# Summing second products over pairs of units, another decoding table, and waits by tile, in a fused attention and two-mixture kernel

## The chip, the cores and the metric

The kernel runs on one core of one Trainium2 chip. The core has five engines with a program of their own each: TensorE (PE in the profile; its weight loads are PEld), VectorE (DVE), ScalarE (ACT), GpSimd (POOL) and SyncE (SP), which issues transfers. What counts is the device time of one execution in microseconds (us), the median over several runs.

## What is computed

An attention over clustered heads gives x (1536 tokens by 512). Two mixtures follow, and the change is in the first:

```python
def _moe_ref(x, w_in, w_out, a, b):      # x 1536 x 512, w_in 512 x 2048, w_out 2048 x 512, weights float64
    h = x @ w_in
    h2 = h * h
    h3 = h2 * h
    P = a[0] + a[1] * h + a[2] * h2 + a[3] * h3
    Q = 1.0 + np.abs(b[0]) * np.abs(h) + np.abs(b[1]) * h2
    g = P / (Q + 1e-06)
    return (g @ w_out).astype(np.float32)
```

The second mixture (`_moe2_ref`) takes that result: a gate over 8 experts, normalised in 8 rounds, then for each expert `relu(x @ w1) @ w2`, weighted by the gate and summed. Every product is made as three matmuls of high and low parts (`mm3`, lines 778 to 781), so that about float32 precision is reached.

## The kernel before, in words

**Stages.** The attention fills the first 287 us of the profiled execution, the first mixture 287 to 581 us, the second mixture the rest. The order of the instructions on each engine is the order in which the Python code issues them; nothing reorders them.

**Units, chunks, ticks.** The 2048 hidden columns of the first mixture are cut into 8 units of 256 (`NU1`). The 1536 tokens are cut into 3 chunks of 512, and a unit's columns into 2 blocks of 128 (`FT`), so each unit has 6 (`PER`) blocks h of 128 x 512, and the mixture 48 (`N1`). The loop over t (lines 1199 to 1239) makes one tick for each: TensorE makes the block h of number n = t (`stage1`, 12 matmuls of 512 columns into a PSUM bank; there are three such banks, pool `ps_1`) and, four ticks behind (`LAG1`), two blocks y of a second product (`stage2`, 6 matmuls each). A tick is thus 24 matmuls. What is issued in which tick stands in the table `plan`, which lines 1157 to 1196 fill.

**The activation.** A block h is read by four ScalarE operations one tick later (`act_b`, lines 820 to 823: h2, q, uu, ww), by two of GpSimd (lines 824 and 825, the polynomial into uu), one of VectorE (`act_q`, L829) and by ScalarE's logarithm and exponentials (`act_r`, lines 833 to 837), which put 1/Q into h's own bank. Another tick later VectorE runs `act_steps`: L843 makes the high part of g (hh), L844 and L847 the residue res, L850 the low part hl. L850 is the last reader of h's bank. For every third n above 3, GpSimd does that last step instead (L848), on a copy rr of the reciprocal.

**The sums.** For each y block of a unit VectorE adds the bank to the accumulator in SBUF (`out1`, L882), two such adds a tick; for unit 0 ScalarE copies (L880). When the last unit has been added, ScalarE and GpSimd split the sum into the high and low parts XH and XL, the second mixture's input.

**Decoding.** The weights come as float64, loaded as pairs of 32-bit words (`load_w`, line 606; one staging buffer for w_in and one for w_out) and decoded into high and low float32 parts by `split_w`. A unit has two weight tiles, (unit, 0) of w_in and (unit, 1) of w_out, each 128 x 1024. Six steps, one per tick, make one tile: a on ScalarE (L649), b on VectorE (L652), c on VectorE (L655), d a copy on ScalarE (L660) and two VectorE operations (L661, L662), e and f on GpSimd (L665, L668). A tile is begun every three ticks, so steps a to c of one tile fall between d to f of the one before.

**The order within a tick** on VectorE is this line, where `outs` are the adds, a, b, c, d the four steps of `act_steps`, and w the decoding step:

```python
            steps = outs[:1] + [a] + firsts + [b] + outs[1:] + [c] + p.get("w", []) + [d]
```

**Pools.** Buffers come from pools that lie on a stack, and a new pool may lie where a closed one lay. The pools of the first mixture (`tp`, `accp`, `hb`, `ps_1`, `ps_2`, `ps_q` and others) are opened after those of the attention are closed.

Of the kernel before, what the change touches and what calls it, by code (L numbers as in the profile page):

```python
# [9 lines left out]
F32 = mybir.dt.float32  # L10
# [23 lines left out]
def kernel(  # L34
# [15 lines left out]
    nc = tc.nc  # L50
# [43 lines left out]
    def left(name, bufs):  # L94
        return ctx.enter_context(tc.tile_pool(name=name, bufs=bufs))
# [577 lines left out]
    LASTK = 2 * NT * (NPR - 1)  # L673
    early = {0: [lambda: (load_w(0, 0), load_w(0, 1))]}
# [28 lines left out]
    tp = mctx.enter_context(tc.tile_pool(name="tp", bufs=2))  # L703
# [4 lines left out]
    sg2 = right(ctx, "sg2", 1)  # L708
    ps_1 = psum(ctx, "ps_1", 3)
# [79 lines left out]
    def stage1(n, ui, c, f):  # L789
        m = units[ui][0]  # L790
        if f == 0:
            hid[ui, c] = (
                hb.tile([P, FT, 512], F32R, tag="hh", name=f"hh_{ui}_{c}"),
                hb.tile([P, FT, 512], F32R, tag="hl", name=f"hl_{ui}_{c}"),
            )
# [43 lines left out]
    def act_steps(n):  # L839
        ps, q0, _, uu, _, gh, gl, *rr = act.pop(n)  # L840
        res = tt("res", n, 2)
# [13 lines left out]

    def stage2(ui, c, i):
        m, e, u = units[ui]
# [3 lines left out]
        if m == 0:  # L861
            first, last = u == 0, u == NU1 - 1
            ps = ps_2.tile([P, 512], F32, tag="2", name=f"y_{ui}_{c}_{i}")
            for f in range(FT):
                mm3(
                    ps, wh[:, f, sl], wl[:, f, sl], gh[:, f], gl[:, f],
                    f == 0, f == FT - 1,
                )
            late.append(lambda: out1(ps, c, i, first, last))
            return  # L870
# [289 lines left out]
    for ui in range(NO):  # L1160
        m = units[ui][0]
        for c in range(NCH):
            for f in range(FT):
                n = ui * PER + c * FT + f
                t = n + m * SHIFT
# [111 lines left out]
```

## Time and profile before

| | |
|---|---|
| median of 3 runs | 1602.87 us (1601.77 to 1603.26) |
| the profiled execution | 1603.93 us |
| its span in the profile | 1602.2 us |
| TensorE busy | 1543.4 us, 96% |
| VectorE busy | 1208.8 us, 75% |
| GpSimd busy | 814.9 us, 51% |
| ScalarE busy | 682.3 us, 43% |

The span is the time from the first to the last recorded instruction; the time of the execution has 1.7 us more around it. In the trace, a group of rows names the line of the code, the engine, and the tiles written and read; a bracket behind an instruction tells how long its engine sat idle before it and which instruction ended that. Matmuls overlap: one of 512 columns is shown with 0.39 us, and the next begins 0.22 to 0.23 us after it.

### The profile page before, as it was taken

The numbers are of one execution on the slowest core, as the hardware profiler recorded it, in microseconds if no ns is written. First come the engines' busy times: TensorE is split into PE (matmuls) and PEld (weight loads), VectorE is DVE, ScalarE is ACT, GpSimd is POOL, SyncE is SP. The second block draws the span as 40 slices with busy tenths as digits, with TensorE's granted clock in tenths as the row PEclk, the third lists the DMA queues.
The fourth block names the chain that finished last, engine by engine and source line by source line (L and its number), as shares of the span: only waits on it lengthen the run. The fifth ranks groups of instructions, "written<-read, shape, count | busy, mean of one in ns | idle before, by whom it ended". The sixth has DMA issues, their size and how long they took to land.

```text
span 1602.2 us, 21123 instructions
## 1 busy us (share of the span) xinstructions
PE 1543.4 (96%) x7780; PEld 1354.3 (85%) x7780; DVE 1208.8 (75%) x1963; ACT 682.3 (43%) x1292; POOL 814.9 (51%) x725
## 2 busy tenths in 40 slices
PE   5999999799999999999999999999999999999999
PEld 4888887577777788889899999989999998999997
DVE  5888888899999966978666766676676666667666
ACT  4999888797777751222221212222121222212121
POOL 5577674698777885243533443353344335334420
PEclk8999999899999999999999999999999999999999
DMA  8555542212112000010110110011011001101102
GB/s 183 135 115 134 132 111 83 74 54 79 53 53 79 14 27 27 27 41 27 40 40 27 40 40 27 27 40 40 27 41 40 27 27 40 40 27 40 40 1 79
DMA packets 70951, 87.96 MB, mean 55 GB/s; under 512 B 29793, under 2 KB 48321, under 8 KB 70849
## 3 DMA queue, kind: packets, MB, share of 16 engines
q1 hardware_dynamic: 70848, 86.63, 19.2%
q8 instruction: 61, 1.00, 0.3%
q14 instruction: 42, 0.34, 0.1%
HBM read 62.97 MB, written 3.19 MB: 41 GB/s over the span
## 4 chain that ended last, share of the span: by engine, by line
PE 77%; DVE 14%; issue 4%; ACT 3%; POOL 2%; DMA 0%; SPq 0%; ACTq 0%; POOLq 0%
PE y L780 12%; PE y L781 12%; PE y L779 12%; PE m L781 9%; PE m L779 9%; PE m L780 9%; PE pt L440 2%; DVE acc L882 2%; PE v L462 2%; PE h L779 1%; PE v L463 1%; PE h L781 1%; PE h L780 1%; DVE ptl L450 1%; PE s L415 1%
## 5 line engine op out<-in xcount | busy, mean ns | idle before, releaser
L896 DVE SCALAR_TENSOR_TENSOR acc<-y,gate,acc 128x512 f32<-128x512 f32 x348 | 260.7, 750 | 189.2 <-PE y L781 188.1
L1013 POOL TENSOR_TENSOR rl<-sg,rh 128x512 fp32r<-128x512 f32 x29 | 45.9, 1584 | 535.4 <-ACT rh L1005 535.4
L781 PE MATMUL y<-wh,gl 128*128 128x512 f32 x696 | 273.1, 392 | 0.0
L780 PE MATMUL y<-wl,gh 128*128 128x512 f32 x696 | 272.8, 392 | 0.0
L779 PE MATMUL y<-wh,gh 128*128 128x512 f32 x696 | 270.6, 389 | 0.0
L1074 ACT ACTIVATE gh<-u 128x384 fp32r<-128x384 f32 x58 | 30.5, 527 | 425.8 <-DVE u L1099 425.8
L781 PEld LDWEIGHTS y<-wh,gl 128*128 128x128 f32 x696 | 130.4, 187 | 27.4
L780 PEld LDWEIGHTS y<-wl,gh 128*128 128x128 f32 x696 | 130.6, 188 | 25.1
L779 PEld LDWEIGHTS y<-wh,gh 128*128 128x128 f32 x696 | 130.7, 188 | 24.7
L779 PE MATMUL h<-XH,wh 128*128 128x512 f32 x264 | 107.0, 405 | 24.3 <-DVE hl L850 24.3
L1090 ACT COPY c<-m 128x384 f32<-128x384 f32 x58 | 27.9, 481 | 220.7 <-PE m L781 220.7
L450 DVE TENSOR_TENSOR ptl<-pt,pth 128x384 fp32r<-128x384 f32 x192 | 97.4, 548 | 29.3 <-ACT pth L449 29.1
L1075 DVE SCALAR_TENSOR_TENSOR gl<-v,gh 128x384 fp32r<-128x384 f32 x174 | 117.1, 673 | 0.0
L1074 ACT ACTIVATE gh<-v 128x384 fp32r<-128x384 f32 x174 | 91.2, 524 | 60.6 <-DVE v L1113 27.5
L781 PE MATMUL h<-XH,wl 128*128 128x512 f32 x264 | 104.4, 395 | 1.1 <-POOL wl L668 1.1
L780 PE MATMUL h<-XL,wh 128*128 128x512 f32 x264 | 104.4, 395 | 0.0
L637 POOL TENSOR_TENSOR wl<-sg,wh 128x512 fp32r<-128x512 f32 x70 | 98.7, 1411 | 5.8
L421 DVE TENSOR_REDUCE nm<-s 128x1 f32<-128x768 f32 x96 | 91.1, 949 | 6.7 <-PE s L416 5.9
L440 PE MATMUL pt<-ident,pr 128*128 128x128 f32 x576 | 85.2, 280 | 8.5 <-DVE ptl L450 8.1
L449 ACT CAST pth<-pt 128x384 fp32r<-128x384 f32 x192 | 82.7, 482 | 23.8 <-PE pt L440 22.7
L429 ACT ACTIVATE pr<-s,nm 128x768 f32<-128x768 f32 x96 | 87.7, 914 | 1.6 <-DVE nm L421 1.1
L824 POOL TENSOR_TENSOR uu<-uu,h 128x512 f32<-128x512 f32 x48 | 67.6, 1409 | 38.5 <-ACT uu L822 38.5
(226 smaller groups left out, 4271.4 us busy)
## 6 DMA issues: line engine op xcount, KB each, us to landing
sg<-in_moe_w_dram SPq DMA_DIRECT2D x64, 512.0 KB, 3.6
stg<-in_moe_w_in_dram SPq DMA_DIRECT2D x8, 1024.0 KB, 5.3
stg<-in_moe_w_out_dram SPq DMA_DIRECT2D x8, 1024.0 KB, 4.8
st<-HQK SPq DMA_DIRECT2D x16, 384.0 KB, 3.9
st<-LQK SPq DMA_DIRECT2D x32, 192.0 KB, 4.3
st<-HQK SPq DMA_DIRECT2D x32, 192.0 KB, 4.5
qk<-in_q_dram SPq DMA_DIRECT2D x16, 192.0 KB, 3.0
qk<-in_k_dram SPq DMA_DIRECT2D x16, 192.0 KB, 3.9
```

The lines of the kernel that those rows point to most:

```text
L421: nc.vector.tensor_reduce(nm, ps[:, :, :HS], axis=AX.XY, op=ALU.max, negate=True)
L429: nc.scalar.activation(pr, ps[:, :, :HS], AF.Exp, bias=nm, accum_out=rss[n][:, x : x + 1])
L440: nc.tensor.transpose(ps[:, i * P : (i + 1) * P], pv_[:, j * P : (j + 1) * P], ident)
L449: nc.scalar.copy(th[:, jj, :], ps[:, :HS])
L450: nc.vector.tensor_tensor(tl[:, jj, :], ps[:, :HS], th[:, jj, :].bitcast(F32), op=ALU.subtract)
L637: gt(wl[:, c], raw[:, c], wh[:, c].bitcast(F32), op=ALU.subtract)
L779: nc.tensor.matmul(ps, ah, bh, start=first, stop=False)
L780: nc.tensor.matmul(ps, ah, bl, start=False, stop=False)
L781: nc.tensor.matmul(ps, al, bh, start=False, stop=last)
L896: nc.vector.scalar_tensor_tensor(a, ps, p, a, op0=ALU.mult, op1=ALU.add)
L1074: nc.scalar.activation(gh[:, f], c, AF.Relu)
L1075: soon.append(lambda: nc.vector.scalar_tensor_tensor(gl[:, f], c, 0.0, gh[:, f].bitcast(F32), op0=ALU.max, op1=ALU.subtract))
```

## The change

1. Every pool that is opened by `left`, `right` and `psum`, and those of the mixture opened directly, get `reuse_waits="tile"`: the first user of a buffer in a new pool then waits for the users of the tiles that lay there, not for those of the whole pool.
2. Units 2 to 7 are taken in pairs, in groups of 12 ticks (`GP`): for each chunk the four h blocks of both units, then the next chunk's. A y block is summed in PSUM over both units, 12 matmuls (`units_sum`), so that there is one y block and one add per tick. Units 0 and 1 stay as they were. A pair's y stand 6 ticks or more behind its h, the last ones in ticks 50 to 53. In tick 54 the second products and the gate's step come before the block h.
3. The table `DECODE` gives for each weight tile the ticks of its six steps, counted from the group's first tick: b and c in one tick, d in the next. The first row is for the first group, the second for the others. From tick 12 on the decoding step comes behind step d of the activation. Decoding ends in tick 37 in place of 41.
4. Buffers: weights have a second pool `wx` for some tiles, the hidden blocks a fourth buffer `hx`, `res` has one buffer in place of two, and the scratch for transfers 1024 in place of 8192 bytes.
5. In the second mixture the gate's factors (`factors`) stand two ticks later, one piece of `pieces_s` one tick later, and the pools `wq` and `cp` are opened at tick 55 instead of 50. The first two weight tiles of the second mixture are split at ticks 46 and 48.

The core of the diff:

```diff
-        return ctx.enter_context(tc.tile_pool(name=name, bufs=bufs))
+        return ctx.enter_context(tc.tile_pool(name=name, bufs=bufs, reuse_waits="tile"))
...
+        pool, bufs = (wx, 1 + i) if ui < NU1 and (ui % 4 > 1 if i else ui % 3 == 2) else (wp, 2)
...
+            pool = hx if m == 0 and len(hid) % 4 == 3 else hb
...
-        res = tt("res", n, 2)
+        res = tt("res", n, 1)
...
+    def units_sum(us, c, i):
+
+        sl = slice(i * P, (i + 1) * P)
+        ps = ps_2.tile([P, 512], F32, tag="2", name=f"y_{us[0]}_{c}_{i}")
+        ks = [(ui, f) for ui in us for f in range(FT)]
+        for ui, f in ks:
+            gh, gl = hid[ui, c]
+            wh, wl = weights[ui, 1]
+            mm3(
+                ps, wh[:, f, sl], wl[:, f, sl], gh[:, f], gl[:, f],
+                (ui, f) == ks[0], (ui, f) == ks[-1],
+            )
+        late.append(lambda: out1(ps, c, i, us[0] == 0, us[-1] == NU1 - 1))
...
+    GP = 2 * PER
+    DECODE = (
+        ((5, 6, 6, 7, 8, 9), (9, 10, 10, 11, 12, 13), (7, 8, 8, 9, 10, 11), (12, 13, 13, 14, 15, 16)),
+        ((3, 4, 4, 5, 6, 7), (8, 9, 9, 10, 11, 12), (6, 7, 7, 8, 9, 10), (11, 12, 12, 13, 14, 15)),
+    )
+    for g in range(NU1 // 2):
+        for x in range(GP):
+            n = t = g * GP + x
+            if g:
+                c, f = divmod(x, 2 * FT)
+                at(t, "s1", (n, 2 * g + f // FT, c, f % FT))
+                at(t - f + 2 * FT + 2 + f, "y", ((2 * g, 2 * g + 1), c, f))
+            else:
+                c, f = divmod(x % PER, FT)
+                at(t, "s1", (n, x // PER, c, f))
+                for i in range(KC * f // FT, KC * (f + 1) // FT):
+                    at(t + LAG1, "y", ((x // PER,), c, i))
+            at(t + 1, "b", n)
+            at(t + 2, "d", n)
+        t = g * GP
+        if g + 1 < NU1 // 2:
+            for when, (ui, i) in zip(DECODE[g > 0], ((2, 0), (3, 0), (2, 1), (3, 1))):
+                at(t + when[0], "P", (2 * g + ui, i, [t + x for x in when]))
...
-            steps = outs[:1] + [a] + firsts + [b] + outs[1:] + [c] + p.get("w", []) + [d]
+            w = p.get("w", [])
+            steps = outs[:1] + [a] + firsts + [b] + outs[1:]
+            steps += [c] + w + [d] if t < GP else [c, d] + w
...
-        for a in p.get("s1", ()):
-            stage1(*a)
+        if t != N1 + 6:
+            firsts_()
         for fn in p.get("g", ()):
             fn()
...
+        seconds()
+        if t == N1 + 6:
+            firsts_()
...
-    for x, fn in zip((3, 3, 4, 4, 5, 6, 7, 8, 8, 9, 10, 11, 12, 13, 14, 15), factors()):
+    for x, fn in zip((5, 5, 6, 6, 7, 8, 9, 10, 10, 11, 11, 12, 13, 14, 15, 16), factors()):
```

How this moves instructions at two places. A row names the line, the operation, the tile written and the tiles read with their numbers, and what the instruction waits for; `DMAHW..` are transfers, the other names engines. First ScalarE at the start of the first mixture, where it goes from the attention's last copy to the first block h; before:

```order
L500 COPY x1f_7_3805<-v_31_3987 64x384
L649 ACTIVATE mag_1_0_4020<-stg_1_0_3902 128x1024 [waits DMAHW3_49]
L820 ACTIVATE h2_0_4076<-h_0_0_0_4063 128x512 [waits DMAHW2_49,DMAHW4_49,DMAHW1_49,DMAHW5_49,DVE_49,DMAHW6_49,PE_49,Pool_49]
L821 ACTIVATE q_0_4079<-h_0_0_0_4063,cf_158 128x512
L822 ACTIVATE uu_0_4077<-h_0_0_0_4063,cf_158 128x512
L823 ACTIVATE ww_0_4078<-h_0_0_0_4063,cf_158 128x512
L833 ACTIVATE h_0_0_0_4063<-q_0_4079,lnb_163 128x512 [waits DVE_49,Activation_49]
```

With the change (line 826 is what line 820 was, and so on):

```order
L500 COPY x1f_7_3805<-v_31_3987 64x384
L650 ACTIVATE mag_1_0_4020<-stg_1_0_3902 128x1024 [waits DMAHW3_49]
L826 ACTIVATE h2_0_4082<-h_0_0_0_4069 128x512 [waits PE_49]
L827 ACTIVATE q_0_4085<-h_0_0_0_4069,cf_158 128x512 [waits Activation_49]
L828 ACTIVATE uu_0_4083<-h_0_0_0_4069,cf_158 128x512
L829 ACTIVATE ww_0_4084<-h_0_0_0_4069,cf_158 128x512
L839 ACTIVATE h_0_0_0_4069<-q_0_4085,lnb_163 128x512 [waits DVE_49,Activation_49]
```

The first activation of block 0 waits for the matmuls alone, where it waited for six transfers, VectorE, GpSimd and TensorE.

Then VectorE in the middle of the mixture, in tick 20 and the start of tick 21 before (q_20 and res_18, res_19 tell the block; y_2_1 and y_2_2 are blocks of unit 2):

```order
L847 TENSOR_TENSOR res_18_5032<-uu_18_4964,q_18_4966 128x512 [waits DVE_49]
L661 TENSOR_SCALAR mag_4_0_4925<-top_4_0_4926 128x1024
L662 SCALAR_TENSOR_TENSOR mag_4_0_4925<-stg_4_0_4769,mag_4_0_4925 128x1024 [waits DVE_49]
L882 TENSOR_TENSOR acc_4059<-y_2_2_0_5070,acc_4059 128x512 [waits PE_49]
L843 TENSOR_TENSOR hh_3_0_4948<-uu_19_5015,h_3_0_1_5001 128x512 [waits Activation_49,Pool_49]
L829 SCALAR_TENSOR_TENSOR q_20_5069<-h2_20_5066,cf_158,q_20_5069 128x512 [waits Activation_49]
L844 SCALAR_TENSOR_TENSOR q_19_5017<-q_19_5017,hh_3_0_4948 128x512 [waits DVE_49]
L882 TENSOR_TENSOR acc_4059<-y_2_2_1_5077,acc_4059 128x512 [waits PE_49]
L847 TENSOR_TENSOR res_19_5091<-uu_19_5015,q_19_5017 128x512 [waits DVE_49]
L652 TENSOR_SCALAR mag_4_1_5086<-mag_4_1_5086 128x1024
L850 TENSOR_TENSOR hl_3_0_4949<-res_19_5091,h_3_0_1_5001 128x512 [waits DVE_49]
L882 TENSOR_TENSOR acc_4059<-y_2_2_2_5126,acc_4059 128x512 [waits PE_49]
```

With the change, two ticks of the same kind of stretch (blocks 26 to 28; lines 653 and 656 are b and c, 662 and 663 are d, 892 the add, 853 res, 856 hl):

```order
L853 TENSOR_TENSOR res_26_5429<-uu_26_5362,q_26_5364 128x512 [waits DVE_49]
L856 TENSOR_TENSOR hl_5_0_5347<-res_26_5429,h_5_0_0_5348 128x512 [waits DVE_49]
L653 TENSOR_SCALAR mag_6_0_5426<-mag_6_0_5426 128x1024
L656 SCALAR_TENSOR_TENSOR top_6_0_5427<-stg_6_0_5175,mag_6_0_5426 128x1024 [waits DMAHW0_49,DVE_49]
L892 TENSOR_TENSOR acc_4065<-y_2_2_2_5467,acc_4065 128x512 [waits PE_49]
L849 TENSOR_TENSOR hh_5_0_5346<-uu_27_5408,h_5_0_1_5394 128x512 [waits Activation_49,Pool_49]
L835 SCALAR_TENSOR_TENSOR q_28_5466<-h2_28_5463,cf_158,q_28_5466 128x512 [waits Activation_49]
L850 SCALAR_TENSOR_TENSOR q_27_5410<-q_27_5410,hh_5_0_5346 128x512 [waits DVE_49]
L853 TENSOR_TENSOR res_27_5480<-uu_27_5408,q_27_5410 128x512 [waits DVE_49]
L662 TENSOR_SCALAR mag_6_0_5426<-top_6_0_5427 128x1024
L663 SCALAR_TENSOR_TENSOR mag_6_0_5426<-stg_6_0_5175,mag_6_0_5426 128x1024 [waits DVE_49]
L892 TENSOR_TENSOR acc_4065<-y_2_2_3_5515,acc_4065 128x512 [waits PE_49]
```

The decoding step has moved behind hl, b and c stand together, and one add stands in a tick instead of two.

## Rows read from the trace of the kernel before

**Rows 1.** The page, part 1: busy time, share of the span, instructions.

```profile
PE 1543.4 (96%) x7780; PEld 1354.3 (85%) x7780; DVE 1208.8 (75%) x1963; ACT 682.3 (43%) x1292; POOL 814.9 (51%) x725
```

**Rows 2.** Busy time by stretch; columns: PE, PEld, DVE, ACT, POOL, clock, DMA share, GB/s.

```profile
336.77:358.53 21.76, 21.76 (x98) 18.02 (x96) 21.00 (x26) 21.57 (x35) 21.45 (x13) 1.00 0.16 49
358.53:542.96 184.43, 170.72 (x722) 134.84 (x721) 183.89 (x241) 138.60 (x212) 147.72 (x92) 0.99 0.17 58
542.96:581.10 38.14, 38.14 (x170) 31.49 (x169) 32.40 (x52) 27.92 (x46) 33.95 (x26) 1.00 0.04 15
690.07:1600.00 909.93, 908.42 (x4543) 820.35 (x4542) 616.39 (x1003) 193.21 (x373) 340.57 (x304) 1.00 0.11 35
```

**Rows 3.** Waits in 287.28 to 581.1: us in total, times, longest.

```profile
PE h L779 <- DVE hl L850: 24.3, 21, 9.5
```

**Rows 4.** TensorE in time: start, duration, operation [idle before <- releaser].

```profile
307.85 0.79 PE L779 MATMUL h<-XH,wh 128*128 128x512 f32 x1 [9.51 <-DVE hl L850]
...
457.49 0.50 PE L779 MATMUL h<-XH,wh 128*128 128x512 f32 x1 [1.34 <-DVE hl L850]
...
463.45 0.50 PE L779 MATMUL h<-XH,wh 128*128 128x512 f32 x1 [0.21 <-DVE hl L850]
...
469.03 0.39 PE L779 MATMUL h<-XH,wh 128*128 128x512 f32 x1
```

**Rows 5.** VectorE in time, ticks of the steady part.

```profile
454.98 1.86 DVE L652 TENSOR_SCALAR mag<-mag 128x1024 uint32<-128x1024 uint32 x1
456.76 0.67 DVE L850 TENSOR_TENSOR hl<-res,h 128x512 fp32r<-128x512 f32 x1
...
459.82 0.67 DVE L882 TENSOR_TENSOR acc<-y,acc 128x512 f32<-128x512 f32 x1
460.42 0.67 DVE L847 TENSOR_TENSOR res<-uu,q 128x512 f32<-128x512 f32 x1
461.01 1.79 DVE L655 SCALAR_TENSOR_TENSOR top<-stg,mag 128x1024 uint32<-128x1024 uint32 x1
462.73 0.67 DVE L850 TENSOR_TENSOR hl<-res,h 128x512 fp32r<-128x512 f32 x1
...
466.97 0.68 DVE L661 TENSOR_SCALAR mag<-top 128x1024 uint32<-128x1024 uint32 x1
467.68 2.20 DVE L662 SCALAR_TENSOR_TENSOR mag<-stg,mag 128x1024 f32<-128x1024 uint32 x1
469.81 0.68 DVE L882 TENSOR_TENSOR acc<-y,acc 128x512 f32<-128x512 f32 x1
```

**Rows 6.** One line's instructions: shortest/median/longest ns, first and last start.

```profile
L655 DVE SCALAR_TENSOR_TENSOR top<-stg,mag x16: 1214/1786/2866, 271.9 to 534.9; 128x1024 uint32<-128x1024 uint32 x16
...
L662 DVE SCALAR_TENSOR_TENSOR mag<-stg,mag x16: 1226/2198/2202, 275.6 to 541.6; 128x1024 f32<-128x1024 uint32 x16
...
L824 POOL TENSOR_TENSOR uu<-uu,h x48: 1270/1308/2271, 299.7 to 576.7; 128x512 f32<-128x512 f32 x48
...
L665 POOL TENSOR_TENSOR top<-top,wh x16: 2358/2402/2859, 278.1 to 546.3; 128x1024 f32<-128x1024 f32 x16
```

**Rows 7.** GpSimd in time, the same part.

```profile
453.89 2.40 POOL L665 TENSOR_TENSOR top<-top,wh 128x1024 f32<-128x1024 f32 x1
```

**Rows 8.** ScalarE, VectorE and GpSimd in time at the mixture's start.

```profile
297.76 0.60 ACT L820 ACTIVATE h<-h 128x512 f32<-128x512 f32 x1 [6.79 <-issue]
...
297.04 0.56 DVE L511 TENSOR_TENSOR XL<-x1f,XH 128x384 fp32r<-128x384 f32 x1
298.94 0.76 DVE L829 SCALAR_TENSOR_TENSOR q<-h,cf,q 128x512 f32<-128x512 f32 x1 [1.35 <-ACT q L821]
...
302.79 0.69 DVE L843 TENSOR_TENSOR hh<-uu,h 128x512 fp32r<-128x512 f32 x1 [2.49 <-POOL uu L825]
...
293.61 2.59 POOL L668 TENSOR_TENSOR wl<-top,mag 128x1024 fp32r<-128x1024 f32 x1
```

**Rows 9.** The page, part 6: loads, KB each, median us to landing.

```profile
stg<-in_moe_w_in_dram SPq DMA_DIRECT2D x8, 1024.0 KB, 5.3
```

More of the change, by code (lines that the diff above doesn't have):

```diff
@@ L708 @@
     sg2 = right(ctx, "sg2", 1)
+    kctx = ctx.enter_context(ExitStack())
+    wx = kctx.enter_context(tc.tile_pool(name="wx", bufs=2, side="right", reuse_waits="tile"))
+    hx = right(kctx, "hx", 1)
     ps_1 = psum(ctx, "ps_1", 3)
@@ L860, in stage2 @@
         sl = slice(i * P, (i + 1) * P)
[L861 to L870, printed above, removed]
         ps = ps_2.tile([P, 512], F32, tag="2", name=f"y_{ui}_{c}_{i}")
@@ L1158, in at @@
         plan.setdefault(t, {}).setdefault(key, []).append(val)
-    for ui in range(NO):
-        m = units[ui][0]
+    GP = 2 * PER
[21 more added lines that the diff above has]
+                at(t + when[0], "P", (2 * g + ui, i, [t + x for x in when]))
+            at(t + (2 if g == 0 else -2), "l", (2 * g + 2, 0))
+            at(t + DECODE[g > 0][0][3], "l", (2 * g + 3, 0))
+            at(t + (5 if g == 0 else 1), "l", (2 * g + 2, 1))
+            at(t + DECODE[g > 0][2][3], "l", (2 * g + 3, 1))
+    for x, fn in enumerate(ahead):
+        at(x + 1, "w", fn)
+    at(2, "P", (1, 1, (2, 3, 4, 5, 6, 7)))
+    at(N1 - 10, "l", (NU1, 0))
+    at(N1 - 7, "l", (NU1, 1))
+    at(N1 - 3, "l", (NU1 + 1, 0))
+    at(N1 - 1, "l", (NU1 + 1, 1))
+    at(N1 - 2, "W", (NU1, 0))
+    at(N1, "W", (NU1, 1))
+    for ui in range(NU1, NO):
         for c in range(NCH):
@@ L1224, with firsts_, seconds @@
         xs.clear()
[L1225 to L1226 removed]
+        def firsts_():
+            for a in p.get("s1", ()):
+                stage1(*a)
+        def seconds():
+            for a in p.get("y", ()):
+                units_sum(*a)
+            for ui, c, f in p.get("s2", ()):
+                for i in range(4 * f // FT, 4 * (f + 1) // FT):
+                    stage2(ui, c, i)
+        if t != N1 + 6:
+            firsts_()
         for fn in p.get("g", ()):
             fn()
[L1229 to L1231 removed]
+        seconds()
+        if t == N1 + 6:
+            firsts_()
+        for ui, i, when in p.get("P", ()):
+            for x, fn in zip(when, split_w(ui, i)):
+                if x > t:
+                    at(x, "w", fn)
+                else:
+                    fn()
         for ui, i in p.get("W", ()):
```

46 lines of the change are left out of this document (20 added, 26 removed).

## The prediction, made before the changed kernel was run

> **What bounds the kernel now.** I read the page's totals first: TensorE is busy 1543.4 us, 96% of the span [rows 1], so some 60 us are all that a change of schedule could win anywhere. The table by stretch says where they lie [rows 2]. From 690.07 us to 1600 TensorE has 908.42 of 909.93 us; nothing is to be had there. In the first mixture it is gapless in 336.77 to 358.53 (ticks 8 to 11) and from 542.96 on (tick 42 and later). The four gapless ticks took 21.76 us, so a tick of 24 matmuls costs TensorE 5.44 us. Ticks 12 to 41 took 184.43 us where 30 times 5.44 is 163.2: **21.2 us are lost there.** In the same stretch VectorE is busy 183.89 of the 184.43 us. VectorE is the bound of this stretch, not TensorE.
>
> The waits agree: in the whole first mixture TensorE's h waits 21 times, 24.3 us, for VectorE's L850 [rows 3], since L850 is the last reader of a PSUM bank that a later h takes. One of the waits is the 9.51 us at 307.85; in the steady ticks it is 1.34, then 0.21, then none [rows 4].
>
> VectorE's clockwork, from start to start: an add at 459.82 to its successor at 460.42, 0.60; L655 at 461.01 to 462.73, 1.72; L652 at 454.98 to 456.76, 1.78; L661 0.71 and L662 2.13 [rows 5]. Decoding one weight tile thus costs VectorE 1.78 + 1.72 + 0.71 + 2.13 = 6.34 us every third tick, although L655 and L662 also ran in 1.21 and 1.23 us [rows 6]. The rest is waiting within the instruction: L652 of 454.98 ends at 456.84, just after GpSimd's L665 (453.89 + 2.40 = 456.29) and a free run of its own [rows 5, 7]. So VectorE's decoding steps and GpSimd's operations here run one after the other. The Trainium skill ("SBUF — State Buffer", Who interferes with whom) says the same as a rule: the port pair that VectorE shares with GpSimd is an exclusive lock, and whoever issues second blocks until the other's instruction is done.
>
> **The adds.** The second products of units 2 to 7 are summed over pairs of units in PSUM, so 36 of 84 adds go, one per tick of those units. In a saturated VectorE each is 0.60 us of its time [rows 5]. The matmuls stay as many, so TensorE's 5.44 per tick stay. VectorE's three ticks are now 3 times 184.43 / 30 = 18.44 us [rows 2]; they become 18.44 - 1.80 = 16.64, against 16.32 on TensorE. If the decoding were spread evenly, 0.32 per three ticks would be lost, 1.3 per 12.
>
> **The decoding table.** It is not even. From tick 12 on, each 12 ticks hold four tiles; L652 and L655 of a tile stand back to back in one tick, L661 and L662 in the next. A tick without decoding costs VectorE (16.64 - 6.34) / 3 = 3.43 on average; one with the first pair 3.43 + 3.50 = 6.93, 1.49 over TensorE's tick; one with the second 3.43 + 2.84 = 6.27, 0.83 over. A tile is 2.32 over, and the tiles come as one (ticks 4, 5 of a group), two in a row (7 to 10), and one (12, 13). Whole, that is 9.3 per 12 ticks, which light ticks make good only as far as TensorE may run ahead of a late VectorE. How far that is, one thing shows: today's heaviest tick (L661, L662) is (18.44 - 6.34) / 3 + 2.84 = 6.87, 1.43 over, and of three ticks only two make TensorE wait [rows 4]; about one such excess is carried. I take **1.4 us of carry**: 0.9 is lost at the first tile, 3.2 at the two in a row, 0.9 at the last, 5.0 and with the rounding of ticks that are not average 5.2 per 12 ticks. The decoding from tick 12 on lies in 28 ticks: 5.2 x 28 / 12 = **12.1 us in place of 21.2**.
>
> Bounds. Below: the lock's own sum. GpSimd per three ticks has six of 1.27 (L824's shortest, L825 alike), L848 at about the same 1.3, L665 and L668 at 2.36 each, 13.6; VectorE's four steps in a free run 0.6 + 1.2 + 0.6 + 1.2 = 3.6, less some 0.1 each of overlap [rows 6, 7]. That is 17.1 against TensorE's 16.32: 0.8, or 3.2 per 12 ticks, 7.5 us in all. Above: nothing carried, 9.3 x 28 / 12 = 21.7. I stand nearer the middle, because of the row with the third tick that doesn't wait. By the Trainium skill's lock taken strictly (same page and section) 7.5 would be the floor and no order of the steps could go under it; the sum above doesn't hang on it.
>
> **Denser start of decoding.** The first group's table is tighter: by tick 11 VectorE has four decoding instructions more behind it than today, while its adds are those of today. In ticks 6 to 11 it has L652 and L655, L661 and L662 by turns, three tiles; by the prices above, and 0.60 or 0.66 for each other instruction, that is 6.56, 5.90, 5.96, 5.90, 7.16 and 6.50 us, 38.0 together, against 6 times 5.44 = 32.6 on TensorE: 5.3 over. Less the carry that is **3.9 us lost**; today TensorE loses nothing in ticks 8 to 11 [rows 2]. Ends: 2.5 (double the carry) and 5.3 (none).
>
> **The start.** ScalarE is free at 290.97 and starts its first L820 at 297.76, 6.79 us later, when VectorE's L511 has ended at 297.60 [rows 8]. It waits for whole pools of the stage before; by the order it then waits for TensorE only, whose h has long been done. Its four operations then end long before GpSimd is free at 293.61 + 2.59 = 296.20; two of GpSimd's 1.27 end at 298.74 [rows 6, 8]. VectorE's q can start at 297.60 rather than 298.94, ScalarE's two on q follow, and L843 comes at some 299.75 instead of 302.79. The step L655 between there and L850 is still to be paid in part, so I take **2.65 us won**; ends 0 (some other release holds ScalarE) and 3.05 (all of it). TensorE's pause of 9.51 stays some 7 us, and the first matmul behind it takes 0.79 us where a later one behind a shorter pause takes 0.50 [rows 4]: that restart stays paid, I count no gain.
>
> **Costed at nothing.** *The third L850 on GpSimd (L848) and one res buffer instead of two*: VectorE's res of the next tick then waits for L848, 1.3 to 1.6 us on GpSimd right after its res; gh, q, the add and q0 stand between (2.4 us), which covers it; if GpSimd is a decoding step late (2.4) VectorE idles 1 to 2 us there, every third tick. *The fourth hidden buffer, the extra weight buffers*: without them units of a pair could not overlap; they add no operation. *Loads*: 1 MB lands in 5.3 us [rows 9] and each is issued two ticks (10.9 us) or more ahead of its first step; SP's order is almost unchanged. *Hand-over*: the last y now stand in ticks 50 to 53, and behind the very last come an add of 0.6, ScalarE's copy of the next stage's input, some 0.6 as L820 [rows 8], and GpSimd's rest of it, 1.3: 2.5 us, in which TensorE has second products of the second mixture (half a tick, 2.7) and the gate's logits. If that cover is gone, 2.5 us. *Factors two ticks later*: in 690 to 1600 no row shows TensorE waiting, so nothing.
>
> **Sum.** 1603.93 (the profiled execution: 1602.2 and 1.7 around it) - 2.65 - (21.2 - 12.1) + 3.9 = 1596.1. I predict **1596**. This execution lies 1.1 above the median of the runs; I don't subtract that, it is below what a measurement can tell. About two tenths of a per cent, 3.2 us, is the least that it can.
>
> **Rivals.**
> 1. *VectorE's waits shrink with the new order, and TensorE is the bound.* L655 right behind L652 may find the port still its own. With the waits halved the heavy ticks are about 6.0 and 5.7, which the carry covers: no loss in ticks 8 to 39, 1603.93 - 21.2 - 2.65 = 1580; with the lock's sum of 3.2 per 12 ticks partly in force up to 1587. Middle 1583. For it: L655 and L662 do run in 1.2 when alone [rows 6]. Against: GpSimd is busy 147.72 of 184.43 us [rows 2], so a free moment is rare. Chance 0.17.
> 2. *The bunched decoding gives the adds back.* With half the carry a group of 12 loses 7.3, 17 in all, the early ticks 4.6: 1601.7. With none: 21.7 and 5.3, 1607.1. Most of what lies between is no change that can be told. For it: the four heavy ticks in a row have no light one between. Chance 0.21; of this 0.03 is faster, 0.14 the same, 0.04 slower.
> 3. *Slower: each second step of a back-to-back pair is locked out once more.* While L652 runs, GpSimd's next operation queues; when it goes first and is L665 or L668 (2.4 us), L655 takes its longest, 2.87 instead of 1.79 [rows 6], 1.08 more per tile. A tile is then 3.4 over, a group loses 2.0 + 5.4 + 2.0 = 9.4 with the carry kept, 22 in all; the early ticks lose 6.1: 1603.93 - 2.65 + 0.8 + 6.1 = 1608.2. It decides from a loss of some 9.9 per group on (23.1 in all, with start and early ticks as in the sum 3.2 above today). For it: today an add or L850 stands between any two steps, so this was never seen in the steady ticks. Against: GpSimd's long two are two in nine of its operations. Chance 0.12, of which 0.09 slower.
> 4. *The pools' waits don't go.* That ScalarE is held by something that the order does not show costs the 2.65 alone, 1598.8; it lies within the main case.
>
> **How the numbers follow.** Main case 0.50, from the lock's floor (21.2 - 7.5 - 2.5 + 2.65 = 13.9, 1590) to some two thirds of the carry (1600). The range leaves out rival 3's 0.12 and half of rival 1's: **1583 to 1605**. Faster: 0.50 + 0.17 + 0.03 = 0.70; slower: 0.09 + 0.04 = 0.13; the rest, 0.17, the same.
>
> **What would show it.** Right: the restart at 307.85 comes 2 to 3 us earlier; adds 48 instead of 84; the span of ticks 12 to 41 shrinks from 184.4 to some 175 us, TensorE's waits for VectorE's hl in it bunched behind ticks 4, 5, 7 to 10, 12 and 13 of each group, with none in the light ticks; ticks 40 and 41 gapless; VectorE no longer full in the stretch. Rival 1: the steps' means fall below 1.5. Rival 3: L655's mean rises above 2.5. Wrong: idle time that ends on GpSimd, or TensorE waiting at the change of mixtures, or any loss after 690 us.

## The result and the profile after

The changed kernel takes 1618.37 us in the median of 4 runs (1616.49 to 1622.89), the kernel before beside it 1602.96: a ratio of 1.0102 (95% interval 1.009 to 1.0115). It is **slower by about 1%**, where 1596 was forecast; the time lies outside the range.

The page of the changed kernel, part 1, answers to [rows 1]:

```profile
PE 1546.6 (96%) x7780; PEld 1357.9 (84%) x7780; DVE 1201.2 (74%) x1927; ACT 682.9 (42%) x1292; POOL 826.2 (51%) x725
```

The table by stretch, cut at the first matmul of ticks 4, 12, 20 and 47 and at the first product of the second mixture's later part (columns as in [rows 2]); first the kernel before:

```profile
287.28:307.85 20.57, 11.06 (x49) 8.83 (x48) 16.49 (x18) 12.99 (x20) 11.70 (x7) 0.86 0.20 66
...
307.85:358.53 50.68, 47.39 (x193) 37.23 (x193) 49.09 (x59) 46.71 (x75) 44.12 (x26) 0.96 0.20 63
358.53:408.05 49.52, 46.54 (x194) 36.70 (x192) 49.26 (x66) 36.87 (x58) 42.80 (x26) 0.97 0.20 64
408.05:570.18 162.13, 151.40 (x648) 120.67 (x649) 157.89 (x212) 121.53 (x187) 128.44 (x84) 1.00 0.15 49
570.18:686.92 116.74, 115.73 (x524) 95.00 (x523) 80.95 (x167) 33.11 (x56) 68.35 (x60) 1.00 0.10 32
```

and the changed kernel:

```profile
285.67:304.99 19.32, 11.06 (x49) 8.82 (x49) 17.76 (x17) 11.89 (x18) 12.04 (x7) 0.86 0.19 68
...
304.99:367.08 62.09, 51.32 (x192) 39.78 (x193) 60.90 (x63) 50.95 (x80) 48.83 (x28) 0.88 0.21 68
367.08:415.40 48.32, 39.89 (x169) 31.07 (x168) 47.49 (x60) 35.42 (x55) 43.93 (x26) 1.00 0.21 66
415.40:574.77 159.37, 152.18 (x649) 123.38 (x648) 140.43 (x180) 122.05 (x189) 132.56 (x82) 0.98 0.12 40
574.77:699.48 124.71, 121.36 (x548) 99.49 (x547) 80.10 (x163) 32.13 (x54) 65.80 (x57) 1.00 0.10 30
699.48:1600.00 900.52, 900.52 (x4513) 814.85 (x4512) 611.54 (x999) 193.40 (x374) 344.56 (x309) 1.00 0.10 34
```

The spans are 12.5 us apart (1614.7 and 1602.2), and the cuts place nearly all of it. The medians are 15.4 apart: the profiled execution of the changed kernel is the fastest of its four, and the one before lies 1 us above its median, so some 3 us of the difference stand in no trace. The mixture begins 1.6 us earlier (285.67 for 287.28). From there to tick 4: 1.25 less. **Ticks 4 to 11: 62.09 in place of 50.68, 11.4 more.** Ticks 12 to 19: 1.2 less, but 24 matmuls of second products (5.44 us) have moved from there to behind tick 47, so 4.2 more for the same work. Ticks 20 to 46: 2.8 less. The last stretch: 8.0 more, less the 5.44 that came to it, 2.5. The sum is -1.6 - 1.25 + 11.4 + 4.2 - 2.8 + 2.5 = 12.5. The first of these can't be told from the spread: the runs below, many with the attention untouched, begin the mixture anywhere from 285.5 to 289.4 us.

Where ticks 4 to 11 lose, TensorE's rows in time show, in the changed kernel:

```profile
304.99 0.79 PE L784 MATMUL h<-XH,wh 128*128 128x512 f32 x1 [8.26 <-DVE hl L856]
...
332.72 0.79 PE L784 MATMUL h<-XH,wh 128*128 128x512 f32 x1 [4.38 <-DVE hl L856]
333.31 0.63 PE L785 MATMUL h<-XL,wh 128*128 128x512 f32 x1
333.73 0.63 PE L786 MATMUL h<-XH,wl 128*128 128x512 f32 x1
...
354.74 0.80 PE L784 MATMUL h<-XH,wh 128*128 128x512 f32 x1 [3.33 <-DVE hl L856]
```

Two pauses of 4.38 and 3.33 us have come that were not there, and each is followed by a stretch at the lower of TensorE's two levels, 1.2 GHz in place of 2.4 (0.63 us a matmul, the next 0.42 behind it, where 0.39 and 0.23 are the rule; the granted clock over ticks 4 to 11 is 0.88). For the same matmuls TensorE is busy 51.32 us in place of 47.39, so 3.9 of the 11.4 are the clock, and 7.5 the waiting. What VectorE and GpSimd did ahead of the first pause:

```profile
327.48 1.30 DVE L653 TENSOR_SCALAR mag<-mag 128x1024 uint32<-128x1024 uint32 x1
328.81 3.25 DVE L656 SCALAR_TENSOR_TENSOR top<-stg,mag 128x1024 uint32<-128x1024 uint32 x1
331.99 0.67 DVE L856 TENSOR_TENSOR hl<-res,h 128x512 fp32r<-128x512 f32 x1
```

```profile
328.19 2.79 POOL L666 TENSOR_TENSOR top<-top,wh 128x1024 f32<-128x1024 f32 x1
330.95 2.26 POOL L830 TENSOR_TENSOR uu<-uu,h 128x512 f32<-128x512 f32 x1
```

L653 holds GpSimd's L666 (2.79 in place of 2.36, [rows 6]) until 328.78; then L666 goes first, and L656 right behind L653 waits it out and takes 3.25, ending at 332.06; and L830, 1.27 alone, is held in turn. That is rival 3, and its size was too small: 3.25 here, not 2.87. It is no single case; over ticks 4 to 19 L656 has a mean of 3.07 us, where its counterpart L655 had 1.79 in the steady ticks:

```profile
L656 DVE SCALAR_TENSOR_TENSOR top<-stg,mag 128x1024 uint32<-128x1024 uint32 x7 | 21.5, 3070 | 0.2
```

The table says one thing more. In ticks 20 to 46 VectorE is busy for 140.43 of 159.37 us, so it is no longer full, and the stretch is still only 2.8 us shorter.

### The profile page after: what moved, and what is told of

It reads as the page before. It is cut to its first block, busy times and chain, and to the rows that moved or that the text cites. A ratio compares the mean times of both kernels' runs of the same rounds, so it can differ in the third digit from the quotient of the medians.

```text
span 1614.7 us, 21096 instructions
## 1 busy us (share of the span) xinstructions
PE 1546.6 (96%) x7780; PEld 1357.9 (84%) x7780; DVE 1201.2 (74%) x1927; ACT 682.9 (42%) x1292; POOL 826.2 (51%) x725
## 4 chain that ended last, share of the span: by engine, by line
PE 77%; DVE 13%; issue 4%; ACT 4%; POOL 2%; DMA 0%; ACTq 0%; DVEq 0%; POOLq 0%
PE y L785 12%; PE y L786 12%; PE y L784 12%; PE m L786 9%; PE m L784 9%; PE m L785 9%; PE pt L440 2%; PE v L462 2%; PE h L784 1%; PE h L786 1%; PE h L785 1%; PE v L463 1%; PE s L415 1%; DVE ptl L450 1%; PE s L416 1%
## 5 line engine op out<-in xcount | busy, mean ns | idle before, releaser
L784 PEld LDWEIGHTS h<-XH,wh 128*128 128x128 f32 x264 | 51.6, 196 | 47.4 <-DVE hl L856 33.3
L830 POOL TENSOR_TENSOR uu<-uu,h 128x512 f32<-128x512 f32 x48 | 73.8, 1538 | 34.1 <-ACT uu L828 34.0
```

The source lines that it names most:

```text
L784: nc.tensor.matmul(ps, ah, bh, start=first, stop=False)
L830: gt(uu, uu, h2, op=ALU.mult)
```

## The experiments

Each run stands beside the kernel before on the same chip; differences are to that. Letters name theories: A, the second step of a back-to-back pair is locked out once more; B or L, the density of the decoding, VectorE's steps and GpSimd's operations one after the other; C, the place of the step ahead of hl (line 850 before, 856 after), but in the run that leaves out adds the loop from a block h over ScalarE, GpSimd and VectorE's hl to the next h; D, ScalarE's wait for a scratch tile.

**Back-to-back steps alone**, in the kernel before:

```diff
-        return [step_a, step_b, step_c, step_d, step_e, step_f]
+        def step_bc():
+            step_b()
+            step_c()
+
+        return [step_a, step_bc, lambda: None, step_d, step_e, step_f]
```

> The kernel before with steps b and c of a weight tile back to back in the tick of b, the rest of the tile's ticks as they are. Theory A: L655's mean rises from 1.79 to 2.8 or more, about 1.1 us per tile on a VectorE that is full, for some ten tiles: 10 to 12 us slower, 1614. Theory B: the same work in the same density, so L655 keeps 1.8 or less and the time stays within 3 us of 1603.

Measured: 1635.1 us, ratio 1.0203 (1.0188 to 1.0219), **32 us slower**. The sign is theory A's, the mechanism is not: it asked for an L655 of 2.8 us or more, and the longest of the run is 2.19. Ticks 20 to 46 of this run, then VectorE's rows and the pause of TensorE:

```profile
422.52:603.68 181.16, 162.47 (x650) 130.90 (x648) 161.52 (x211) 121.88 (x187) 133.51 (x84) 0.92 0.14 44
```

```profile
495.47 1.87 DVE L652 TENSOR_SCALAR mag<-mag 128x1024 uint32<-128x1024 uint32 x1
497.38 2.17 DVE L655 SCALAR_TENSOR_TENSOR top<-stg,mag 128x1024 uint32<-128x1024 uint32 x1
499.47 0.68 DVE L854 TENSOR_TENSOR hl<-res,h 128x512 fp32r<-128x512 f32 x1
...
506.20 0.69 DVE L886 TENSOR_TENSOR acc<-y,acc 128x512 f32<-128x512 f32 x1 [1.68 <-PE y L785]
```

```profile
500.20 0.57 PE L783 MATMUL h<-XH,wh 128*128 128x512 f32 x1 [2.67 <-DVE hl L854]
```

The steps grew only a little (L655 2.17 in place of 1.79; it met a GpSimd operation of 1.41 us there, not one of 2.4). But they now fall into one tick: hl is late by both, TensorE pauses 2.67 us in place of 1.34 [rows 4], its clock falls, and in the light tick that follows VectorE waits for TensorE (1.68), so nothing is made good. TensorE's busy time for the same matmuls is 162.47 in place of 151.40: **11.1 of this stretch's 19.0 us are the lower clock** behind pauses. Another 14.1 us were lost in ticks 4 to 19 (114.26 in place of 100.20).

**Half of the adds alone**: the kernel before with 30 of its 84 adds left out (those of y blocks 1 and 3 of units 2 to 6; its sums lack these blocks).

```diff
-            late.append(lambda: out1(ps, c, i, first, last))
+            if u < 2 or i % 2 == 0 or last:
+                late.append(lambda: out1(ps, c, i, first, last))
```

> The kernel before with every second add of units 2 to 6 left out (y blocks i = 1 and 3 of these units are never added; their matmuls are still made), nothing else changed: what the adds alone are worth in the old order. By the prediction's reasoning VectorE's three ticks fall from 18.44 to 17.1 or less, so ticks 12 to 41 lose some 8 to 13 us less: 1592. If the waits come from the loop h, ScalarE, GpSimd, VectorE's hl, next h, in which the adds hardly stand (theory C): 1600 or more, as the changed kernel won only 2.8 us in ticks 20 to 47.

Measured: 1601.9 beside 1603.5, ratio 0.9989 (0.9979 to 0.9998): **1.6 us for 30 adds**, where 0.60 each would be 18. Groups of VectorE by line over 18 ticks, in the kernel before and in this run:

```profile
L882 DVE TENSOR_TENSOR acc<-y,acc 128x512 f32<-128x512 f32 x37 | 25.0, 676 | 0.0
...
L652 DVE TENSOR_SCALAR mag<-mag 128x1024 uint32<-128x1024 uint32 x6 | 11.2, 1869 | 0.0
L655 DVE SCALAR_TENSOR_TENSOR top<-stg,mag 128x1024 uint32<-128x1024 uint32 x6 | 10.7, 1785 | 0.0
```

```profile
L652 DVE TENSOR_SCALAR mag<-mag 128x1024 uint32<-128x1024 uint32 x6 | 15.7, 2625 | 0.0
L655 DVE SCALAR_TENSOR_TENSOR top<-stg,mag 128x1024 uint32<-128x1024 uint32 x6 | 13.5, 2251 | 0.0
...
L883 DVE TENSOR_TENSOR acc<-y,acc 128x512 f32<-128x512 f32 x19 | 12.9, 678 | 0.0
```

The adds lost 12.1 us of busy time, and the two steps took 7.3 of it back: L652 came earlier to the same running operation of GpSimd and waited longer for it. One such tick of this run, VectorE and GpSimd:

```profile
472.16 2.63 DVE L652 TENSOR_SCALAR mag<-mag 128x1024 uint32<-128x1024 uint32 x1
474.71 0.68 DVE L850 TENSOR_TENSOR hl<-res,h 128x512 fp32r<-128x512 f32 x1
```

```profile
471.85 2.40 POOL L665 TENSOR_TENSOR top<-top,wh 128x1024 f32<-128x1024 f32 x1
```

L665 ends at 474.25 and hl begins 0.46 us later; before it was 456.29 and 0.47 later [rows 5, 7]. So hl, for which TensorE waits, hung on GpSimd's operation and not on the adds, as the expectation's theory C has it (1600 or more). VectorE looks as full as ever (181.70 of 183.08 us in ticks 12 to 41). This is the run that overturns the prediction's first reading.

**The waits by tile alone**, in the kernel before (all pools, nothing else).

> The kernel before with nothing but the waits by tile in place of the waits for whole pools. Both theories of the slowdown (A: the second of two decoding steps back to back is locked out for a whole GpSimd operation once more; B: the earlier and denser decoding that the pairs need costs it, in whatever order the steps stand) have the waits outside of it: the first block h and the restart of tick 4 come 1.6 and 2.9 us earlier, as in the changed kernel, and nothing else moves: 1600.1 us, 2.9 less than before. If the gain at the start is eaten again by VectorE being the bound behind it: 1603.

Measured: 1602.07 beside 1602.74, ratio 0.9995 (0.9985 to 1.0004), no change that can be told. From the first h to tick 4 it took 18.52 us (286.37 to 304.89) in place of 20.57; ticks 4 to 11 gave 0.9 of that back (51.62). What is left does not show in the medians.

**The late factors alone**, in the kernel before (the two `zip` rows of the change, nothing else; ten of the sixteen pieces stand two ticks later in them, six one tick).

> The kernel before with nothing but the second mixture's factors two ticks later (and one piece one tick later). If that causes the longer waits of the gate's rounds (3.35 us in place of 1.01): 2.3 to 2.5 us more, 1605.4, with a wait of 2 to 3 us at one of the rounds. If these waits come from the pairs' late end: 1603 and a longest wait of about 1 us.

Measured: 1607.45, ratio 1.0028 (1.0018 to 1.0038), 4.7 us slower. TensorE's waits in the gate's rounds, of the kernel before, this run and the changed kernel:

```profile
PE sk L768 <- DVE gate L764: 1.0, 1, 1.0
```

```profile
PE sk L768 <- DVE gate L764: 3.4, 2, 2.8
```

```profile
PE sk L773 <- DVE gate L769: 3.3, 2, 2.8
```

The same waits come from this part of the change alone; in the changed kernel they are the 2.5 us of the last stretch. Alone the part costs more: from tick 47 to the end 4.2 us (1036.1 in place of 1032.0). There TensorE's pause of 2.78 us was followed by its lower level (granted clock 0.59 from 650.8 to 655.0); in the changed kernel a pause of 2.76 at the same place was followed by full speed (1.00 from 662 to 670). **The factors one tick earlier in the changed kernel**, so one late instead of two, was to give some of it back:

> The changed kernel with the second mixture's pools opened at tick 54 and the factors one tick earlier, so one tick later than in the kernel before instead of two. If the meeting of factors and gate rounds in one tick is what costs 2.5 to 4.7 us: half or more of it comes back, 1614 to 1616, and TensorE's longest wait for the gate falls below 2 us. Else 1618.

It did not: 1622.65, ratio 1.0126 (1.0109 to 1.0142).

```profile
PE sk L773 <- DVE gate L769: 4.2, 1, 4.2
...
PE lg L733 <- POOL XL L1267: 1.8, 1, 1.8
```

A round of the gate waits longer than before (4.2), and TensorE is at its lower level behind it (granted clock 0.50 from 660 to 665). GpSimd's XL, for which the logits wait, stands behind a factor and the split of a weight tile. So the cost does not simply grow with the number of ticks; it depends on what the factors meet.

**Spreading the steps** in the changed kernel: step b and the first half of d behind q, the others as they were; first in ticks 0 to 11, then in all (`then` marks these steps).

```diff
+            for fn in p.get("w", []):
+                if hasattr(fn, "then") and (t < GP):
+                    ahead_w.append(fn)
...
-            steps = outs[:1] + [a] + firsts + [b] + outs[1:]
+            steps = outs[:1] + [a] + firsts + ahead_w + [b] + outs[1:]
```

> The changed kernel with one change: in ticks 0 to 11 step b, and the first VectorE operation of step d, stand ahead of L850's place (behind q) instead of directly ahead of the other operation of their pair; tables, pairs, density stay. Theory A: the second operations take 1.8 to 2.2 again instead of 3.3, ticks 4 to 20 lose some 8 to 10 us less: 1609. Theory B: density is what costs, so 1617 to 1619.

> As the run that spread the steps in ticks 0 to 11, now in all ticks: step b, and the first VectorE operation of d, behind q, the others behind hl from tick 12 on. Theory A: the steps' means fall below 1.9 in ticks 12 to 37 and these lose less than the 22 us of the changed kernel by some 5: 1617 (the run with the first group spread gave 1622.3). Theory C: b now stands ahead of hl again, so nothing is won or some 5 us are lost: 1622 to 1627.

Measured: 1622.34, ratio 1.0133 (1.0107 to 1.0158), and 1618.36, ratio 1.0095 (1.0078 to 1.0112). Neither gave anything back. In the first, L656 still had a mean of 2.58 us in ticks 4 to 11 (2.90 in the changed kernel), so the spread alone did not bring the steps down to the 1.8 to 2.2 that theory A asked for. In the second, ticks 12 to 46 took 4.3 us less, but ticks 4 to 11 took 5.1 more. **Steps behind hl** in ticks 0 to 11 of the changed kernel (`[c, d] + w` in all ticks):

> The changed kernel with the decoding steps of ticks 0 to 11 behind hl (L856's place) as in all later ticks, instead of directly ahead of it; the tables and the density stay. Theory C: the pair's 3.5 to 4.5 us no longer delay the instruction for which TensorE waits, and ticks 4 to 20 lose 8 to 15 us less: 1603 to 1610. Theories A and B: VectorE has the same work in the same density with the same steps back to back: 1617 to 1619.

Measured: 1621.71, ratio 1.0115 (1.01 to 1.013). Taken alone, against theory C. But all three runs showed a wait that had been overlooked: ScalarE's step a, of which the changed kernel has 6.4 us from 300 to 420 us and these runs 9.4 to 11.5.

**A scratch tile of its own** for weight tiles (2,1) and (3,0) takes that wait away:

```diff
-        mag = dp.tile(shape, F32, tag="mag", name=f"mag_{ui}_{i}")
+        if (ui, i) in ((2, 1), (3, 0)):
+            mag = sg2.tile(shape, F32, tag=f"sg{i}", name=f"mag_{ui}_{i}")
+        else:
+            mag = dp.tile(shape, F32, tag="mag", name=f"mag_{ui}_{i}")
```

> The changed kernel with one change: the scratch tile mag of weight tiles (2,1) and (3,0) lies in buffers that are free then (the second mixture's staging), so that ScalarE's step a need not wait for GpSimd's step f of the tile two before; order and tables stay. Theory D (ScalarE, with the next block's operations queued behind that wait, starves GpSimd and VectorE): the waits of L650 for L669, 6.4 us in the changed kernel, go, and ticks 4 to 20, which lose 36.8, lose 6 to 9 less: 1611. Theory L (VectorE's pairs and GpSimd's operations one after the other are simply more than the ticks hold where tiles stand two ticks apart): 0 to 2 less, 1617.

> The run with all steps spread, with the same change to mag. There L650 waited 11.5 us for GpSimd, up to 5.6 at once. Theory D: all of that comes back, 1618.4 - 11 = 1607. Theory L: 1616 to 1618.

> The run with the steps of ticks 0 to 11 behind hl, with the same change to mag. There L650 waited 9.4 us. Theory D: 1621.7 - 9 = 1613, or less if the place behind hl then pays. Theory L: 1620.

Measured: 1617.45 (ratio 1.0089, 1.0074 to 1.0104), 1613.03 (1.0067, 1.005 to 1.0084) and 1615.69 (1.0081, 1.0066 to 1.0096). ScalarE's wait in that part in the changed kernel (us in total, times, longest), and with its own scratch alone:

```profile
ACT mag L650 <- POOL wl L669: 6.4, 3, 3.9
```

```profile
ACT mag L653 <- POOL wl L672: 1.6, 1, 1.6
```

Alone the scratch is worth nothing that can be told (1617.45 and 1618.37); the likely reading is that ScalarE's wait lies in the shadow of VectorE's pairs. Where the pairs are spread or stand behind hl, it is worth 5 to 6 us. Two waits covered each other, and the runs that undid one of them at a time misled. The third run shows it by stretch: with steps behind hl and the scratch, ticks 4 to 11 took 55.48 in place of 62.09, as theory C asked, and ticks 12 to 19 gave most of it back (53.59 in place of 48.32). With pairs and scratch wait both gone (1613.03), the changed kernel is still 10 us slower than before.

**Density.** Left out of the changed kernel: the decoding of unit 3's two weight tiles (unit 3 computes with unit 2's); first as it is, then with steps spread and own scratch.

> The changed kernel without the decoding of unit 3's two weight tiles (unit 3 takes unit 2's): two tiles out of the four that stand in ticks 5 to 16, on all engines. Theory B (density): ticks 4 to 20, which lose 36.8 us in the changed kernel and 22.1 before, fall to 22 or less, so 1603. Theory C (the place ahead of hl in the tick): what is left still stands ahead of hl, each pair costs its own, so half of the 14.7 comes back: 1611. Theory A asks the same as C here.

> The run with steps spread and mag of its own, now without the decoding of unit 3's two weight tiles (unit 3 takes unit 2's): neither pairs of steps nor four tiles in ticks 5 to 16. Theory L (density: tiles two ticks apart are more than VectorE's steps and GpSimd's operations, one after the other, get into the ticks): ticks 4 to 20 lose 8 us less, 1605. If something else of the change is what is left there (a single res buffer, the pairs of units): 1611 or more.

Measured: 1619.42 (1.0101, 1.0085 to 1.0116) and 1612.94 (1.0066, 1.0051 to 1.0081). There is no gain in the sum, but the sum misleads. Ticks 4 to 19, then 20 to 46, of the run with steps spread and own scratch, and of the same without unit 3's tiles:

```profile
305.69:410.67 104.98, 90.16 (x361) 70.89 (x361) 99.80 (x122) 86.68 (x134) 95.70 (x52) 0.94 0.22 71
410.67:568.88 158.21, 150.58 (x649) 122.14 (x648) 135.91 (x180) 122.77 (x189) 136.04 (x83) 0.99 0.13 41
```

```profile
306.37:404.12 97.75, 88.26 (x361) 69.99 (x361) 88.53 (x114) 82.56 (x130) 79.73 (x48) 0.96 0.23 76
404.12:568.62 164.50, 154.49 (x650) 124.34 (x648) 137.51 (x180) 122.58 (x189) 135.11 (x83) 0.97 0.12 39
```

Where the tiles are missing 7.2 us are won, near the 8 of theory L; behind it 6.3 are lost. The same in the first run: ticks 4 to 19 took 105.53 in place of 110.41, ticks 20 to 46 took 164.44 in place of 159.37. The loss is made by the omission itself. ScalarE's step d of tick 22, in the first run and in the second:

```profile
435.71 1.05 ACT L661 CAST wh<-top 128x1024 fp32r<-128x1024 f32 x1 [10.57 <-PE h L785]
```

```profile
427.30 1.05 ACT L664 CAST wh<-top 128x1024 fp32r<-128x1024 f32 x1 [9.07 <-PE h L792]
```

By the code, units 2 and 5 share one buffer of `wx` for w_in; since unit 3 reads unit 2's tile here, the copy for unit 5 has to wait for unit 3's last block h, and ScalarE stands 9 to 11 us that the changed kernel does not have. So these runs don't speak against theory L. They don't prove it either: they take away work that the kernel before has in these ticks too. So the reverse was tried, **denser starts alone** in the kernel before, one step per tick as ever, (2,1), (3,0) and (3,1) started 1, 1 and 2 ticks earlier (and the scratch mag of (2,1) and (3,0) in free buffers, as above):

```diff
-                at(max(0, t + x), "W", (ui + 1, i))
+                at({(2, 1): 7, (3, 0): 10, (3, 1): 12}.get((ui + 1, i), max(0, t + x)), "W", (ui + 1, i))
```

> The kernel before with only the starts of three weight tiles moved ahead: (2,1) in tick 7 in place of 8, (3,0) in 10 in place of 11, (3,1) in 12 in place of 14 (mag of two of them in free buffers), one step per tick as before: the density of the changed kernel's first group without its pairs of steps. Theory L: ticks 4 to 20 lose 4 to 8 us more, of which ticks 14 to 20 give some back: 1605 to 1609. If density costs nothing without the pairs: 1603.

Measured: 1607.42, ratio 1.0028 (1.0016 to 1.004), 4.6 us slower. TensorE's first new pause and the step ahead of it:

```profile
350.61 0.80 PE L782 MATMUL h<-XH,wh 128*128 128x512 f32 x1 [3.15 <-DVE hl L853]
```

```profile
342.25 1.78 DVE L655 TENSOR_SCALAR mag<-mag 128x1024 uint32<-128x1024 uint32 x1
...
346.52 3.43 DVE L658 SCALAR_TENSOR_TENSOR top<-stg,mag 128x1024 uint32<-128x1024 uint32 x1
349.88 0.68 DVE L853 TENSOR_TENSOR hl<-res,h 128x512 fp32r<-128x512 f32 x1
```

GpSimd, at the same time as L658:

```profile
346.50 2.38 POOL L668 TENSOR_TENSOR top<-top,wh 128x1024 f32<-128x1024 f32 x1
```

Ticks 4 to 11 took 55.45 in place of 50.68 there (ticks 4 to 19 together 105.28 in place of 100.20): density costs by itself, and again in one late hl with a pause of TensorE behind it. No step stands right ahead of this L658, and it takes 3.43 us all the same, while the second steps of the steady pairs above took 2.17. What makes a step long is that it meets GpSimd's operation of 2.4 us; a pair is one way to that.

**One res buffer alone**, in the kernel before:

> The kernel before with one res buffer in place of two. By the prediction's step it is covered: 1603. If VectorE's res then waits for GpSimd's L848 on the way to hl: 0.5 to 1.5 us per period of three ticks, 1608 to 1615.

Measured: 1602.48, ratio 0.9998 (0.9989 to 1.0008): nothing, as costed. In the changed kernel's first mixture, too, no res waits for GpSimd's hl.

**The step behind hl in the kernel before**, with waits by tile:

```diff
-            steps = outs[:1] + [a] + firsts + [b] + outs[1:] + [c] + p.get("w", []) + [d]
+            steps = outs[:1] + [a] + firsts + [b] + outs[1:] + [c, d] + p.get("w", [])
```

> The kernel before with waits by tile and the decoding step behind L850 instead of ahead of it. If the step's place ahead of the instruction that TensorE waits for is what costs (theory C): ticks 12 to 41 lose 5 to 10 us less, 1594. Theory L: the same operations one after the other in the same three ticks, 1601 to 1603.

Measured: **1597.7 beside 1602.8, ratio 0.997 (0.9958 to 0.9981): faster than both kernels.** Its table from tick 4, 12 and 20 on:

```profile
304.29:355.87 51.58, 48.27 (x193) 38.35 (x193) 48.97 (x60) 47.66 (x76) 43.67 (x26) 0.93 0.19 62
355.87:404.74 48.87, 44.80 (x193) 35.72 (x192) 48.59 (x65) 36.67 (x58) 41.68 (x26) 1.00 0.20 65
404.74:563.92 159.18, 149.48 (x649) 120.97 (x648) 154.57 (x213) 122.94 (x189) 128.80 (x85) 1.00 0.15 50
```

Ticks 20 to 46 are 159.18, as in the changed kernel (159.37), with all 84 adds: moving the one step won there as much as the whole change did. L652's median fell with it, from 1.85 to 1.12 us. The other 3 us lie ahead of tick 4 (17.51 us from the first h, in place of 20.57; waits by tile alone had 18.52), less 0.9 in ticks 4 to 11. The time lies between the expectations of C and L. **The same with half of the adds left out** (the same blocks as above):

> The kernel before with waits by tile and the decoding step behind L850 (1597.7 us), now with every second add of units 2 to 6 left out as in the run that left them out alone. If the adds are worth nothing because GpSimd's operations and the decoding steps, one after the other, set the period: 1596 to 1598. If VectorE's own time is the bound once the step no longer stands ahead of hl: 7 us or more less, 1590.

Measured: 1594.69, ratio 0.995 (0.9935 to 0.9964): 3.0 less than with all adds (3.4 against the kernels before beside them), 0.1 per add. That lies between its two expectations as well. In either order an add is worth a small part of its 0.60.

## Why the prediction was wrong

**The first step failed: "VectorE is the bound of this stretch."** It was read from 183.89 of 184.43 us busy [rows 2]. The prediction itself saw that L652, L655 and L662 wait within their busy time, and then took that busy time as a load that shrinks by 0.60 with each add. It doesn't: 30 adds less were worth 1.6 us, since the steps only waited longer for the same GpSimd operation, and hl came when that operation had ended. Ticks 12 to 46 were to win 9.1 and lost 1.5 (4.2 more, then 2.8 less): 22.7 us over TensorE's own time (5.44 for each 24 matmuls) in place of 21.2. That is the size of rival 2's end without any carry (21.7) and of rival 3 (22), so the number does not choose between them; against rival 2, VectorE is no longer full in ticks 20 to 46.

**The carry of 1.4 us** was read from the third tick of [rows 4]. The run with back-to-back steps does not show it: a heavy tick's lateness reaches TensorE, and VectorE is idle in the light tick, waiting for TensorE. What was missing as well is the price of a pause: "that restart stays paid, I count no gain" was right for the old one, but a new pause can have a restart of its own, 3.9 us of clock in ticks 4 to 11 and 11.1 in the stretch of the paired steps.

**The denser start** was costed at 3.9 us with ends of 2.5 and 5.3; ticks 4 to 11 lost 11.4. Alone, without pairs, denser starts cost 4.6. Undoing the pairs (rival 3: L656 at 3.25) and the scratch wait of ScalarE behind them gave 5.3 back, of which 3.2 in ticks 4 to 11 (58.92 in place of 62.09).

**"Factors two ticks later, so nothing"** looked only behind 690 us. The factors moved within the gate's rounds, ahead of it, and cost 4.7 alone and 2.5 in the changed kernel.

**The start** was worth 1.25 us from the first h to tick 4 in the changed kernel and 2.05 alone, where 2.65 was taken; of the 2.05, 0.9 were given back in ticks 4 to 11. **Right** were the res buffer, the loads and the hand-over to the second mixture (no wait for a transfer from the first h on, and none of TensorE behind tick 47 but the gate's 3.3), and that nothing is lost behind the first mixture and the gate (TensorE is busy all of the 900.52 us from 699.48 on).

**Rival 3** named the wait and the right sign, with a chance of 0.12 and 1608.2. Its 22 us from tick 12 on came out (22.7); its 6.1 for the early ticks were 11.4. It saw the wait in the second step of a pair only; a step met GpSimd's long operation without a pair too, ScalarE's wait for the scratch stood behind it, and the clock came on top (3.9 of the 11.4).

**A sum** of the prediction does not come out: the lock's own sum is 13.6 + 3.6 less four times 0.1, that is 16.8 and not 17.1, so the floor was 4.5 us and not 7.5. It shifts an end of the main case and of rival 1, and nothing in the forecast.

Apart, by stretch of the profiled executions: ticks 4 to 19 lost 15.6 us (11.4 and 4.2). Undoing pairs and scratch wait took 5.4 of it away (110.41 to 104.98), and denser starts cost 5.1 alone. If the two add up, 5 are left, and these are not settled. No run has the pairs of units, the buffers `wx` and `hx`, the smaller scratch for transfers or the order of tick 54 alone.

## What to carry to other kernels

An engine that is busy all the time is not the bound while part of its busy time is waiting for another engine: before costing a removed instruction at its duration, look whether a lengthened neighbour will take the time back. Work that can be held up by another engine is better placed behind the instruction that the matmuls wait for than ahead of it: that won 5.1 us in the kernel before, with waits by tile, though in the changed kernel it won at most 2, and only once ScalarE's scratch wait was gone (1615.69 and 1617.45). A pause of TensorE costs itself and can cost slower matmuls after it, so work that is even can beat work that is bunched with the same sum: two steps in one tick cost 32 us. When two waits may cover each other, undo both before giving up either.

## What the runs showed of the hardware that was not expected

A VectorE step of 1.2 us took up to 3.43 when it met a GpSimd operation of 2.4, and that GpSimd operation up to 3.40 in the changed kernel when it met VectorE's (2.79 in the rows above): both are held, in turn, and the busy columns of both engines rise with it. The Trainium skill ("SBUF — State Buffer", Who interferes with whom) says that the one that issues first keeps the shared port pair for its whole instruction; the rows around 328 us agree (L666 waits out L653, then L656 waits out L666). That the waiting stands within the busy time of these rows is what misled the prediction. After pauses of 2.67, 3.33 and 4.38 us TensorE's next matmuls ran at the lower level (0.63 us each, granted clock 0.88 over ticks 4 to 11); where pauses of 2.67 came in every third tick, the mean clock of a whole stretch was 0.92. The length alone does not tell: after the 2.76 us in the gate's rounds of the changed kernel the clock stayed at 1.00, after 2.78 at the same place in the run of the late factors it was 0.59. The steady pauses of 1.34 us before left it at 1.00.
